# An attention and mixture-of-experts kernel: the weight splits of the first expert in another order around the routing's end, and one running count formed earlier

## The chip, the cores and the metric

One core of a Trainium2 chip runs the whole program. The metric is the device time of one execution in microseconds (us), the median of three runs. For this kernel a change of about 0.2% (1.5 us) is what a measurement can tell from none.

## The reference, cut to what matters

Attention with capped scores feeds a dense layer with SoLU and layer norm, and that feeds a layer of eight experts of which each token uses one. Only the last part lies near the change:

```python
def _moe2_ref(x, modality_id, w_gate, modality_bias, w1, w2):
    logits = x @ w_gate + modality_bias[modality_id]      # x: 1792 x 768, 8 experts
    e_idx = np.argmax(logits, axis=1)
    probs = softmax(logits)
    gate_w = probs[np.arange(N), e_idx]
    for e in range(E):
        mask = e_idx == e
        h = np.maximum(x[mask] @ w1[e], 0.0)              # w1[e]: 768 x 1024
        out[mask] = gate_w[mask, None] * (h @ w2[e])      # w2[e]: 1024 x 768
```

## The kernel before, in words

The 1792 tokens are 14 tiles of 128 (t = 0 to 13). Each tile goes through the dense layer: `m_h` (L590 to L592), `m_act`, `m_tr`, then `m_y` (L645 to L647), which gives y and, in eight more columns, the logits `lg` (L649). `m_out` stores y to `ysc` in memory. Float32 products are made of three passes of TensorE over a high and a low part of each operand. A weight therefore has to be loaded, cast to its high part on ScalarE (`act.copy`) and subtracted to its low part on VectorE (`dve.tensor_sub`); this is called a split.

When the first ten tiles have logits, the expert with most tokens so far is picked (`route_early`), two slots of 128 of its tokens are gathered, and this first expert E is computed while the last tiles are still being routed. Its weights come through `e_weights(w)` (L1021): w = 0 are six blocks of w1, into `winh` and `winl`, w = 1 are eight blocks of w2, into `wouh` and `woul`. Every step of that generator issues one load into a ring of three buffers `e_raw` from SyncE's queue, the cast and the subtraction. The ring makes load k + 3 wait until the subtraction of block k is done. `e_h` (L1032) is the first product of E: 144 matmuls into `e_ph`, with a relu on ScalarE (`e_hh`, L1050) and a low part on VectorE (`e_hl`, L1051) after each quarter of its last pass. `e_o` (L1056) is its second product, into `e_po` (L1063 to L1065).

Meanwhile the routing of tiles 10 to 12 and of tile 13 runs in two generators of `route_group`: a one-hot `r_oh` of each token's expert, a count before each token (matmuls into `pr`), the running count `cum`, the counts of each expert (`route_total`, `route_counts`), then tables of tokens, `route_expert` and `route_end`, which writes `eidx` (the expert of each later slot), `gidx` and `sidx` (its tokens). After that the slots D, H and so on follow (`run_slots`). Their weights are loaded into `raw_D` (a ring of four) on the same queue of SyncE, behind the loads of `e_raw`. The expert index of the first of them is read from `eidx` on SyncE. Between the blocks of `e_o`, TensorE transposes D's gathered tokens (`xtD`, L1209, two buffers in PSUM), which ScalarE and VectorE split (`xh_D` L1210, `xl_D` L1211).

The order on TensorE and VectorE is written out by hand in this part (`manual_schedule`); ScalarE's and SyncE's is chosen by the framework at build time. Each engine executes its list in order. The hand-written order around the change is this (`run` takes steps of the dense layer, `run_h` steps of `e_h`, `ra` and `rb` are the two routings):

```python
        run(3)
        next(rb)
        next(ee["w0"])
        run(4)
        late_w = e_weights(1)
        eh = e_h()
        for k in EHS:
            run_h(k)
            next(rb, None)
            next(late_w)
        for _ in late_w:
            pass
```

Of the kernel before, what the change touches and what calls it, by code (L numbers as in the profile page):

```python
# [12 lines left out]
F16 = mybir.dt.float16  # L13
I32 = mybir.dt.int32
AF = mybir.ActivationFunctionType
ALU = mybir.AluOpType
# [5 lines left out]
NT, DM, DF, NE = 1792, 768, 1024, 8  # L22
P = 128
# [33 lines left out]
PEND0 = 17  # L57
QH = (6, 6)
RDEL = 4
EHS = (8, 22, 20)  # L60
ETD = 8
LSEP = (10, 12)
TRP = (4, 0, 0)
# [23 lines left out]
def attn_moe_kernel(ctx, tc, qt, kt, vv, cap, w_in, w_out, g_ln, ids, w_gate, mbias, w1, w2, out):  # L87
# [164 lines left out]
    def route_group(K, tp, psR, atile, a, b):  # L252
        n = b - a
        oh = K["oh"][:, a:b, :]
        kk = tp.tile([P, n, NE], F32, name=f"kk{a}")
        dve.tensor_tensor(kk, lg[:, a:b, :], nmx[:, a:b].unsqueeze(2).to_broadcast([P, n, NE]), op=ALU.add)
        dve.scalar_tensor_tensor(kk, kk, 0.0, K["rev"][:, a:b, :], op0=ALU.is_equal, op1=ALU.mult)
        fm = tp.tile([P, n], F32, name=f"fm{a}")
        dve.tensor_reduce(fm, kk, axis=AX.X, op=ALU.max)
        dve.tensor_tensor(oh, kk, fm.unsqueeze(2).to_broadcast([P, n, NE]), op=ALU.is_equal)  # L260
        pr = atile(f"pr{a}")[:, 0, :n * NE].rearrange("p (t e) -> p t e", e=NE)
        prev = rstate.get("cum")
        last = b == NTILE
        yield
        mm = []
        if prev is not None:
            mm.append((pr, K["ones"], prev.unsqueeze(1).to_broadcast([P, n, NE])))
        for t in range(n - 1):
            mm.append((pr[:, t + 1:, :], K["ones"], oh[:, t:t + 1, :].to_broadcast([P, n - 1 - t, NE])))
        pe.matmul(pr, K["tri"], oh, start=True, stop=not mm)  # L270
        for i, (o, l, r) in enumerate(mm):
            pe.matmul(o, l, r, start=False, stop=(i == len(mm) - 1))
        cum = tp.tile([P, NE], F16, name=f"cum{a}")
        if n == 1:
            dve.tensor_tensor(cum, prev, oh[:, 0, :], op=ALU.add)
        else:
            cs = tp.tile([P, NE], F32, name=f"cs{a}")
            dve.tensor_reduce(cs, oh.rearrange("p t e -> p e t"), axis=AX.X, op=ALU.add)
            if prev is None:
                dve.tensor_copy(cum, cs)  # L280
            else:
                dve.tensor_tensor(cum, cs, prev, op=ALU.add)
        rstate["cum"] = cum
        if last:
            route_total(K)
        pm = tp.tile([P, n, NE], F32, name=f"pm{a}")
        dve.tensor_tensor(pm, pr, oh, op=ALU.mult)
        if last:
            yield
            route_counts(K, tp)  # L290
            yield
        rf = tp.tile([P, n], F32, name=f"rf{a}")
        dve.tensor_reduce(rf, pm, axis=AX.X, op=ALU.add)
        ri, pl, ph = (tp.tile([P, n], I32, name=f"{x}{a}") for x in ("ri", "pl", "ph"))
        dve.tensor_copy(ri, rf)
        dve.tensor_scalar(pl, ri, P - 1, None, op0=ALU.bitwise_and)
        dve.tensor_scalar(ph, ri, 7, None, op0=ALU.logical_shift_right)
        A, Bm = K["A"][:, a:b, :], K["B"][:, a:b]
        dve.tensor_tensor(A, K["io128"].unsqueeze(1).to_broadcast([P, n, P]),
                          pl.unsqueeze(2).to_broadcast([P, n, P]), op=ALU.is_equal)  # L300
        rm = tp.tile([P, n, NR], F16, name=f"rm{a}")
        dve.tensor_tensor(rm, K["io14"].unsqueeze(1).to_broadcast([P, n, NR]),
                          ph.unsqueeze(2).to_broadcast([P, n, NR]), op=ALU.is_equal)
        dve.tensor_tensor(rm, rm, K["tid"][:, a:b].unsqueeze(2).to_broadcast([P, n, NR]), op=ALU.mult)
        dve.tensor_tensor(Bm, oh.unsqueeze(3).to_broadcast([P, n, NE, NR]),
                          rm.unsqueeze(2).to_broadcast([P, n, NE, NR]), op=ALU.mult)
        if last:
            route_expert(K, tp)
        else:
            yield  # L310
        if a == 0:
            rstate["pt"] = psR.tile([NE * NR, P], F32, name="r_pt")
        for t in range(a, b):
            pe.matmul(rstate["pt"], K["B"][:, t].rearrange("p a b -> p (a b)"), K["A"][:, t, :],
                      start=(t == 0), stop=(t == b - 1), skip_group_check=True)
        if a == 0:
            route_early(K, tp, psR)
        if last:
            yield
            route_end(K, tp)  # L320

    def route_early(K, tp, psR):

# [38 lines left out]
    def route_counts(K, tp):  # L362
        sm = rstate["sm"]
        c8 = tp.tile([NE, 1], F32, name="r_c8")
        dve.scalar_tensor_tensor(c8, rstate["s8"], -float(P), sm[:NE, 0:1], op0=ALU.mult, op1=ALU.add)

        wn = K["wn"]
        dv = tp.tile([NE, 2], F32, name="r_dv")
        nst = tp.tile([NE, 24], F32, name="r_nst")
        for o, lo, hi in ((dv[:, 0:1], 21, 24), (dv[:, 1:2], 14, 21), (wn[:, 6:7], 0, 14)):  # L370
            dve.tensor_scalar(nst[:, lo:hi], K["thr"][:, lo:hi], c8, None, op0=ALU.is_lt, op1=ALU.add, accum_out=o)
        dve.tensor_scalar(wn[:, 7:8], dv[:, 0:1], 4.0, None, op0=ALU.mult)
        dve.tensor_scalar(wn[:, 5:6], dv[:, 1:2], 2.0, None, op0=ALU.mult)
        dve.scalar_tensor_tensor(wn[:, 8:9], dv[:, 0:1], -4.0, wn[:, 5:6], op0=ALU.mult, op1=ALU.add)
        dve.tensor_tensor(wn[:, 9:10], wn[:, 6:7], wn[:, 5:6], op=ALU.subtract)
        dve.scalar_tensor_tensor(wn[:, 10:11], wn[:, 6:7], float(P), c8, op0=ALU.mult, op1=ALU.is_lt)
        dve.tensor_scalar(wn[:, 1:2], dv[:, 0:1], -4.0, None, op0=ALU.mult)
        dve.tensor_copy(wn[:, 4:5], wn[:, 7:8])
        r1, k = wn[:, 7:11], NE * NR
        leq = K["leq"].rearrange("p a b -> p (a b)")  # L380
        pe.matmul(sm[:NE, 8:12], K["lin"], r1, start=True, stop=True)
        pe.matmul(sm[:k, 60:64], K["lex"].rearrange("p a b -> p (a b)"), r1, start=True, stop=False)
        pe.matmul(sm[:k, 60:64], leq, wn[:, 0:4], start=False, stop=True)
        pe.matmul(sm[:k, 64:67], leq, wn[:, 4:7], start=True, stop=True)
        pe.matmul(sm[:1, 72:76], K["one8"], r1, start=True, stop=True)

    def route_expert(K, tp):
        sm = rstate["sm"]
        cmp_ = tp.tile([NE, len(KINDS), NK], F16, name="r_cmp")
        sh = [NE, len(KINDS), NK]  # L390
        dve.tensor_tensor(cmp_, K["io8"], sm[:NE, 8:12].unsqueeze(2).to_broadcast(sh), op=ALU.is_ge)
        pe.matmul(sm[:1, 16:16 + NS], K["ones"][:NE, 0:1], cmp_.rearrange("p a b -> p (a b)"), start=True, stop=True)

    def route_end(K, tp):
        sm = rstate["sm"]
# [11 lines left out]
        t4 = tp.tile([k, 4, TT], F16, name="r_t4")  # L407
        dve.tensor_copy(t4, rstate["pt"][:, :TT].unsqueeze(1).to_broadcast([k, 4, TT]))
        dve.tensor_scalar(eidx, sm[:1, 16:16 + NS], float(NE - 1), None, op0=ALU.min)
        pg, pq = sm[:, 128:128 + NG], sm[:, 192:192 + NK]  # L410
        pe.matmul(pg, tt, selg[:, :NG], start=True, stop=True)
        pe.matmul(pq, t4.rearrange("p a b -> p (a b)"), selg[:, NG:], start=True, stop=True)
# [608 lines left out]
    def e_weights(w):  # L1021

        src, rows, width, hs, ls = ((w1r, DM, DF, winh, winl), (w2r, DF, DM, wouh, woul))[w]
        for k in range(rows // P):
            raw = rt.tile([P, DF], F32, tag="e_raw", name=f"e_raw{w}_{k}", bufs=3)[:, :width]
            sp.dma_start(out=raw, in_=src[ds(ee["reg"] * rows + k * P, P), :])
            h_, l_ = hs[k][:, :width], ls[k][:, :width]
            act.copy(h_, raw)
            dve.tensor_sub(l_, raw, h_)
            yield  # L1030
# [59 lines left out]
    def run(k):  # L1090
        for _ in range(k):
            msteps.pop(0)[1]()

    def run_h(k):
        for _ in range(k):
            next(eh)

    with tc.manual_schedule(engines={ET.PE, ET.DVE}):
        run(4)
        ra, rb = (route_group(K, rt, psR, atile, *x) for x in groups)  # L1100
        next(ra)
        next(ee["w0"])
        run(5)
        next(ra)
        next(ee["w0"])
        run(3)
        next(rb)
        run(3)
        next(ra, None)
        next(ee["w0"])  # L1110
        run(3)
        next(rb)
        next(ee["w0"])
        run(4)
        late_w = e_weights(1)
        eh = e_h()
        for k in EHS:
            run_h(k)
            next(rb, None)
            next(late_w)  # L1120
        for _ in late_w:
            pass
        for _ in eh:
            pass
    for pl_ in (rt, xp, wi, psR):
        pl_.release()
# [469 lines left out]
```

## Time and profile before

| | |
|---|---|
| time, median of 3 runs | 757.17 us (757.06 to 757.83) |
| time of the profiled execution | 758.1 us |
| its span (first to last instruction) | 756.4 us |
| TensorE (PE) busy | 725.8 us, 96% |
| VectorE (DVE) busy | 437.8 us, 58% |
| ScalarE (ACT) busy | 387.1 us, 51% |
| GpSimd (POOL) busy | 116.9 us, 15% |
| moved by DMA | 97.14 MB, mean 128 GB/s |

Between the span and the time of the profiled execution lie 1.7 us in which no instruction of the program runs. Busy time of TensorE includes stretches at half its clock, so a stretch that is busy throughout may still be slow.

### The profile page before, as it was taken

To read this page: it belongs to the slowest core of one execution; us is meant where nothing else is said; L and a number is where in the kernel's file an instruction comes from. 1 tells how busy PE (TensorE), PEld (TensorE's weight loads), DVE (VectorE), ACT (ScalarE), POOL (GpSimd) and SP (SyncE) were. 2 spreads that over 40 slices of the span, in tenths; PEclk is the share of its full clock that TensorE was granted. 3 is DMA by queue.
4 is the path that set the end of the run, shared out by engine and by line. 5 is a ranking of instruction groups with operands and counts; after the bars stand their busy time and mean duration, and the time that the engine had idled before them with its cause. 6 is when DMAs were issued, how large, how long until landed. Compare 5 with 4: busy or idle time off the path is not lost. (4 is left out here: it accounts for less than half of the span.)

```text
span 756.4 us, 11328 instructions
## 1 busy us (share of the span) xinstructions
PE 725.8 (96%) x4302; PEld 558.9 (74%) x4302; DVE 437.8 (58%) x782; ACT 387.1 (51%) x535; POOL 116.9 (15%) x214
## 2 busy tenths in 40 slices
PE   5999999999999999999999998969999999999994
PEld 2443556667767777677698998968879998799983
DVE  7999656756656657555457557546146173563621
ACT  5999756774575555555612234244055162643530
POOL 4221101111021112020032111302210220002010
PEclk9999999999999999999999999979999999999998
DMA  8775121121121110110004012648918359484520
GB/s 290 253 237 197 61 59 43 59 73 43 38 83 37 57 58 13 59 34 13 21 22 148 22 50 98 203 184 301 390 58 273 117 184 404 193 266 171 199 104 23
DMA packets 33426, 97.14 MB, mean 128 GB/s; under 512 B 4903, under 2 KB 11057, under 8 KB 33362
## 3 DMA queue, kind: packets, MB, share of 16 engines
q1 hardware_dynamic: 26546, 66.88, 26.2%
q0 software_dynamic: 6528, 29.42, 11.0%
q8 instruction: 35, 0.57, 0.3%
q14 instruction: 29, 0.24, 0.1%
q10 hardware_dynamic: 288, 0.03, 0.0%
HBM read 85.24 MB, written 11.27 MB: 128 GB/s over the span
## 5 line engine op out<-in xcount | busy, mean ns | idle before, releaser
L730 ACT ACTIVATE e<-sc,sc 112x896 f32<-112x896 f32 x96 | 94.5, 1005 | 67.3 <-PE sc L723 67.3
L735 ACT ACTIVATE e<-e,cap_t 112x896 f32<-112x896 f32 x96 | 98.1, 1045 | 1.7
L765 PE MATMUL av<-e,v 112*64 112x448 f32 x384 | 82.8, 552 | 0.0
L645 PE MATMUL y<-wouh,lh 128*128 128x392 f32 (+1 forms) x224 | 77.9, 348 | 1.6 <-DVE lg L649 1.6
L647 PE MATMUL y<-wouh,ll 128*128 128x392 f32 (+1 forms) x224 | 75.8, 338 | 0.2 <-DVE ll L635 0.2
L646 PE MATMUL y<-woul,lh 128*128 128x392 f32 (+1 forms) x224 | 75.9, 339 | 0.0
L590 PE MATMUL h<-winh,xh 128*128 128x512 f32 x168 | 69.0, 411 | 0.0
L592 PE MATMUL h<-winh,xl 128*128 128x512 f32 x168 | 66.0, 393 | 1.1 <-DVE xl L578 1.1
L591 PE MATMUL h<-winl,xh 128*128 128x512 f32 x168 | 65.6, 390 | 0.0
L645 PEld LDWEIGHTS y<-wouh,lh 128*128 128x128 f32 x224 | 42.0, 188 | 10.3 <-issue 7.1
L765 PEld LDWEIGHTS av<-e,v 112*64 112x64 f32 x384 | 23.3, 136 | 35.4 <-issue 33.4
L1179 DVE TENSOR_TENSOR wl_H<-raw_H,wh_H 128x768 fp32r<-128x768 f32 (+1 forms) x28 | 29.2, 1069 | 32.2 <-ACT wh_H L1178 32.2
L590 PEld LDWEIGHTS h<-winh,xh 128*128 128x128 f32 x168 | 31.6, 188 | 16.4 <-issue 9.3
L1308 PE MATMUL poD<-wh_D,hhD 128*128 128x384 f32 x128 | 43.0, 336 | 0.0
L1309 PE MATMUL poD<-wl_D,hhD 128*128 128x384 f32 x128 | 42.8, 334 | 0.0
L1310 PE MATMUL poD<-wh_D,hlD 128*128 128x384 f32 x128 | 42.8, 334 | 0.0
L647 PEld LDWEIGHTS y<-wouh,ll 128*128 128x128 f32 x224 | 42.1, 188 | 0.8 <-DVE ll L635 0.8
L646 PEld LDWEIGHTS y<-woul,lh 128*128 128x128 f32 x224 | 42.1, 188 | 0.6
L1178 ACT CAST wh_H<-raw_H 128x768 fp32r<-128x768 f32 (+1 forms) x28 | 25.3, 941 | 32.5 <-PE phD L1236 14.1
L1179 DVE TENSOR_TENSOR wl_D<-raw_D,wh_D 128x768 fp32r<-128x768 f32 (+1 forms) x28 | 29.6, 1071 | 18.8 <-ACT wh_D L1178 18.5
L592 PEld LDWEIGHTS h<-winh,xl 128*128 128x128 f32 x168 | 31.5, 188 | 8.8 <-DVE xl L578 2.0
L723 PE MATMUL sc<-qr,kr 64*112 64x448 f32 x128 | 30.4, 601 | 7.8 <-DMA qr<-in_qt_dram 7.8
(373 smaller groups left out, 1604.7 us busy)
## 6 DMA issues: line engine op xcount, KB each, us to landing
rawc<-in_w_out_dram POOLq DMA_DIRECT2D x16, 384.0 KB, 4.1
rawc<-in_w_in_dram POOLq DMA_DIRECT2D x12, 512.0 KB, 4.7
raw_D<-in_w_dram SPq DMA_DIRECT2D x12, 512.0 KB, 5.0
wr_T<-in_w_dram SPq DMA_DIRECT2D x16, 384.0 KB, 6.4
raw_D<-in_w_dram SPq DMA_DIRECT2D x16, 384.0 KB, 5.9
wr_T<-in_w_dram SPq DMA_DIRECT2D x12, 512.0 KB, 7.8
raw_H<-in_w_dram SPq DMA_DIRECT2D x12, 512.0 KB, 5.7
raw_H<-in_w_dram SPq DMA_DIRECT2D x16, 384.0 KB, 3.7
```

Of the source, the lines that this page charges most:

```text
L590: pe.matmul(o, s["xh"][d], winh[d][:, c], start=(d == 0), stop=False)
L591: pe.matmul(o, s["xh"][d], winl[d][:, c], start=False, stop=False)
L592: pe.matmul(o, s["xl"][d], winh[d][:, c], start=False, stop=(d == ND - 1))
L645: pe.matmul(o, s["lh"][f], wouh[f][:, c], start=(f == 0), stop=False)
L646: pe.matmul(o, s["lh"][f], woul[f][:, c], start=False, stop=False)
L647: pe.matmul(o, s["ll"][f], wouh[f][:, c], start=False, stop=(f == NF - 1))
L730: act.activation(e, t[:CK, :, :S], AF.Tanh, scale=sc8[:CK])
L735: act.activation(e, e, AF.Exp, scale=cap_t[:CK])
L765: pe.matmul(o[64 * j:64 * j + 64, :S], v[:, c, 64 * j:64 * j + 64], et[b, p, c][:, j, :], start=(c == 0), stop=(c == 3))
L1179: dve.tensor_sub(l_, raw, h_)
L1308: pe.matmul(p, hh[:, f, o], wh[:, c], start=(f == 0), stop=False)
L1309: pe.matmul(p, hh[:, f, o], wl[:, c], start=False, stop=False)
```

## The change

It does two things. The running count of tile 13 is formed right behind its one-hot, before the routing's first stop, and not after the matmuls that follow. And the steps of the weight splits are taken at other places: the generators of w1 and w2 become one (`weights`), the last three splits of w1 are taken later, w2's first four at or behind the stops of the routing's end, and the other four behind `e_h`. The routing's end has new stops: the sums of `route_counts` are a function of their own (`route_sums`), the matmul of `route_expert` comes after a stop, and `route_end` stops before its two matmuls. `EHS` is now pairs of (steps of `e_h`, splits).

```diff
-EHS = (8, 22, 20)
+EHS = ((8, 1), (16, 1), (18, 3))
...
         last = b == NTILE
+        cum = tp.tile([P, NE], F16, name=f"cum{a}")
+        if n == 1:
+            dve.tensor_tensor(cum, prev, oh[:, 0, :], op=ALU.add)
         yield
...
-        cum = tp.tile([P, NE], F16, name=f"cum{a}")
-        if n == 1:
-            dve.tensor_tensor(cum, prev, oh[:, 0, :], op=ALU.add)
-        else:
+        if n > 1:
...
             yield
-            route_counts(K, tp)
+            r1 = route_counts(K, tp)
             yield
+            route_sums(K, r1)
...
         if last:
-            route_expert(K, tp)
-        else:
-            yield
+            cmp_ = route_expert(K, tp)
+        yield
+        if last:
+            pe.matmul(rstate["sm"][:1, 16:16 + NS], K["ones"][:NE, 0:1], cmp_.rearrange("p a b -> p (a b)"), start=True, stop=True)
...
         if last:
-            yield
-            route_end(K, tp)
+            yield from route_end(K, tp)
...
         dve.tensor_scalar(eidx, sm[:1, 16:16 + NS], float(NE - 1), None, op0=ALU.min)
+        yield
...
+    def weights():
+        yield from ee["w0"]
+        yield from e_weights(1)
...
+        ew = weights()
         next(ra)
-        next(ee["w0"])
+        next(ew)
         run(5)
         next(ra)
-        next(ee["w0"])
         run(3)
         next(rb)
+        next(ew)
         run(3)
         next(ra, None)
-        next(ee["w0"])
         run(3)
         next(rb)
-        next(ee["w0"])
+        next(rb)
+        next(ew)
         run(4)
-        late_w = e_weights(1)
         eh = e_h()
-        for k in EHS:
-            run_h(k)
+        for steps, subs in EHS:
+            run_h(steps)
             next(rb, None)
-            next(late_w)
-        for _ in late_w:
+            for _ in range(subs):
+                next(ew)
+        for _ in eh:
             pass
-        for _ in eh:
+        for _ in ew:
             pass
```

What becomes of it on VectorE where the logits of tile 13 arrive, before and then after the change (`winl3` is the low part of w1's block 3, `e_xl` that of E's tokens, the digits behind an underscore are buffers):

```order
L1029 TENSOR_TENSOR winl3_132<-e_raw0_3_4254,winh3_126 128x1024
L649 SCALAR_TENSOR_TENSOR lg_78<-y13_4215,sm13_4106,bias_t_76 128x8
L651 TENSOR_REDUCE nmx_92<-lg_78 128x1
L256 TENSOR_TENSOR kk13_4269<-lg_78,nmx_92 128x8
L257 SCALAR_TENSOR_TENSOR kk13_4269<-kk13_4269,r_rev_3549 128x8
L259 TENSOR_REDUCE fm13_4272<-kk13_4269 128x1
L260 TENSOR_TENSOR r_oh_3615<-kk13_4269,fm13_4272 128x8
L1011 TENSOR_TENSOR e_xl_4277<-e_xt0_4278,e_xh_4276 128x6x128
...
L1029 TENSOR_TENSOR winl4_133<-e_raw0_4_4308,winh4_127 128x1024
L275 TENSOR_TENSOR cum13_4323<-cum10_4235,r_oh_3615 128x8
```

```order
L654 SCALAR_TENSOR_TENSOR lg_78<-y13_4216,sm13_4106,bias_t_76 128x8
L656 TENSOR_REDUCE nmx_92<-lg_78 128x1
L256 TENSOR_TENSOR kk13_4265<-lg_78,nmx_92 128x8
L257 SCALAR_TENSOR_TENSOR kk13_4265<-kk13_4265,r_rev_3549 128x8
L259 TENSOR_REDUCE fm13_4268<-kk13_4265 128x1
L260 TENSOR_TENSOR r_oh_3615<-kk13_4265,fm13_4268 128x8
L266 TENSOR_TENSOR cum13_4272<-cum10_4211,r_oh_3615 128x8
L1034 TENSOR_TENSOR winl3_132<-e_raw0_3_4274,winh3_126 128x1024
L1016 TENSOR_TENSOR e_xl_4279<-e_xt0_4280,e_xh_4278 128x6x128
```

The logits and the running count `cum13` now stand ahead of the subtraction of w1's block 3, and block 4's has gone to a later place.

On VectorE at the end of `e_h`, before and after (`woul0` to `woul7` are w2's eight blocks, `wl0_D0_0` is the first block of D's weights):

```order
L1029 TENSOR_TENSOR woul4_147<-e_raw1_4_4483,wouh4_139 128x768
L1029 TENSOR_TENSOR woul5_148<-e_raw1_5_4487,wouh5_140 128x768
L1029 TENSOR_TENSOR woul6_149<-e_raw1_6_4491,wouh6_141 128x768
L1029 TENSOR_TENSOR woul7_150<-e_raw1_7_4495,wouh7_142 128x768
L1051 SCALAR_TENSOR_TENSOR e_hl0_4348<-e_ph0_4350,e_hh0_4346 128x512 x2
L1051 SCALAR_TENSOR_TENSOR e_hl1_4349<-e_ph1_4386,e_hh1_4347 128x512 x2
L1179 TENSOR_TENSOR wl0_D0_0_4662<-raw0_D0_0_4651,wh0_D0_0_4661 128x1024
```

```order
L1034 TENSOR_TENSOR woul3_146<-e_raw1_3_4471,wouh3_138 128x768
L1056 SCALAR_TENSOR_TENSOR e_hl0_4358<-e_ph0_4360,e_hh0_4356 128x512 x2
L1056 SCALAR_TENSOR_TENSOR e_hl1_4359<-e_ph1_4397,e_hh1_4357 128x512 x2
L1034 TENSOR_TENSOR woul4_147<-e_raw1_4_4585,wouh4_139 128x768
L1034 TENSOR_TENSOR woul5_148<-e_raw1_5_4589,wouh5_140 128x768
L1034 TENSOR_TENSOR woul6_149<-e_raw1_6_4593,wouh6_141 128x768
L1034 TENSOR_TENSOR woul7_150<-e_raw1_7_4597,wouh7_142 128x768
L1189 TENSOR_TENSOR wl0_D0_0_4662<-raw0_D0_0_4651,wh0_D0_0_4661 128x1024
```

The subtractions of blocks 4 to 7 have moved behind the four low parts `e_hl`; blocks 0 to 3 stand ahead of them.

On ScalarE at the same place, before and after:

```order
L1028 CAST wouh5_140<-e_raw1_5_4487 128x768
L1028 CAST wouh6_141<-e_raw1_6_4491 128x768
L1028 CAST wouh7_142<-e_raw1_7_4495 128x768
L1050 ACTIVATE e_hh0_4346<-e_ph0_4350 128x512 x2
L1050 ACTIVATE e_hh1_4347<-e_ph1_4386 128x512 x2
L1178 CAST wh0_D0_0_4661<-raw0_D0_0_4651 128x1024
```

```order
L1033 CAST wouh5_140<-e_raw1_5_4589 128x768
L1033 CAST wouh6_141<-e_raw1_6_4593 128x768
L1055 ACTIVATE e_hh0_4356<-e_ph0_4360 128x512 x2
L1055 ACTIVATE e_hh1_4357<-e_ph1_4397 128x512 x2
L1033 CAST wouh7_142<-e_raw1_7_4597 128x768
L1188 CAST wh0_D0_0_4661<-raw0_D0_0_4651 128x1024
```

Only the cast of block 7 has moved behind the relus `e_hh`; those of blocks 4 to 6 stand ahead of them as before. On SyncE the eight loads of w2 still stand ahead of D's loads `raw_D`; the reading of `eidx` has moved from behind load 4 to ahead of load 3.

## Rows read from the trace of the kernel before

**Rows 1.** TensorE's waits over the span: us in total, times, longest.

```profile
PE e_po L1063 <- ACT e_hh L1050: 6.1, 1, 6.1
PE y L645 <- DVE lg L649: 1.6, 1, 1.6
PE poH L1310 <- PEq L1548: 1.1, 1, 1.1
...
PE r_sm L360 <- DVE cum L275: 1.1, 1, 1.1
```

**Rows 2.** Timeline of TensorE: start, us, work, idle before it and its releaser.

```profile
491.59 0.28 PE L1047 MATMUL e_ph<-e_xh,winl 128*128 128x256 f32 x1
497.98 0.69 PE L1063 MATMUL e_po<-wouh,e_hh 128*128 128x384 f32 x1 [6.12 <-ACT e_hh L1050]
...
511.08 1.01 PE L1209 MATMUL xtD<-ident,ygD 128*128 128x128 f32 x6 [0.62 <-DVE xl_D L1211]
```

**Rows 3.** Stretches: busy of PE, PEld, DVE, ACT, POOL; granted clock, DMA share, GB/s.

```profile
491.80:498.00 6.20, 0.09 (x2) 0.02 (x1) 2.45 (x3) 2.79 (x4) 0.00 (x0) 0.69 1.02 370
498.00:504.40 6.40, 6.31 (x23) 5.80 (x24) 2.41 (x4) 1.19 (x2) 0.00 (x0) 0.50 0.32 127
504.40:506.60 2.20, 2.20 (x16) 2.20 (x15) 0.47 (x1) 1.10 (x2) 0.00 (x0) 0.99 0.00 0
...
496.70:500.30 3.60, 2.23 (x7) 1.72 (x8) 1.56 (x2) 1.23 (x2) 0.00 (x0) 0.50 0.90 360
```

**Rows 4.** Timeline of ScalarE, 491 to 509 us.

```profile
491.60 0.83 ACT L1028 CAST wouh<-e_raw 128x768 fp32r<-128x768 f32 x1 [7.85 <-DMA e_raw<-in_w_dram]
...
496.60 0.83 ACT L1028 CAST wouh<-e_raw 128x768 fp32r<-128x768 f32 x1 [3.01 <-DMA e_raw<-in_w_dram]
497.34 0.59 ACT L1050 ACTIVATE e_hh<-e_ph 128x512 fp32r<-128x512 f32 x1
...
505.99 2.93 ACT L1178 CAST wh_D<-raw_D 128x1024 fp32r<-128x1024 f32 x3
```

**Rows 5.** Timeline of VectorE, 467 to 512 us.

```profile
467.67 1.22 DVE L1029 TENSOR_TENSOR winl<-e_raw,winh 128x1024 fp32r<-128x1024 f32 x1
...
480.09 0.16 DVE L398 TENSOR_TENSOR r_at<-r_sm,r_ck 112x4 f32<-112x4 f32 x1 [1.26 <-PE r_sm L392]
...
481.37 0.17 DVE L409 TENSOR_SCALAR eidx<-r_sm 1x32 int32<-1x32 f32 x1
...
484.36 2.69 DVE L1029 TENSOR_TENSOR woul<-e_raw,wouh 128x768 fp32r<-128x768 f32 x3
...
498.34 0.68 DVE L1051 SCALAR_TENSOR_TENSOR e_hl<-e_ph,e_hh 128x512 fp32r<-128x512 f32 x1
...
506.13 0.69 DVE L1051 SCALAR_TENSOR_TENSOR e_hl<-e_ph,e_hh 128x512 fp32r<-128x512 f32 x1 [2.76 <-ACT e_hh L1050]
507.06 3.50 DVE L1179 TENSOR_TENSOR wl_D<-raw_D,wh_D 128x1024 fp32r<-128x1024 f32 x3 [0.24 <-ACT wh_D L1178]
510.48 1.01 DVE L1211 TENSOR_TENSOR xl_D<-xtD,xh_D 128x384 fp32r<-128x384 f32 x2
```

**Rows 6.** Issues on SyncE's queue (block 5, block 7, D's first); POOL's first gather.

```profile
485.35 0.33 SPq L1026 DMA_DIRECT2D e_raw<-in_w_dram  x1
...
487.08 1.62 SPq L1026 DMA_DIRECT2D e_raw<-in_w_dram  x1
488.91 0.84 SPq L1165 DMA_DIRECT2D raw_D<-in_w_dram  x1
...
483.27 1.10 POOL L1187 DMA_INDIRECT ygD<-ysc,gidx  x1 [5.72 <-DVE r_sf L416]
```

**Rows 7.** Single loads, KB and us to landing, issued at 473.3, 485.4 and 508.3.

```profile
e_raw<-in_w_dram SPq DMA_DIRECT2D x1, 384.0 KB, 2.9
...
e_raw<-in_w_dram SPq DMA_DIRECT2D x1, 384.0 KB, 6.2
...
raw_D<-in_w_dram SPq DMA_DIRECT2D x1, 512.0 KB, 3.5
```

More of the change, by code (lines that the diff above doesn't have):

```diff
@@ L378, in route_counts, with route_sums @@
         dve.tensor_copy(wn[:, 4:5], wn[:, 7:8])
-        r1, k = wn[:, 7:11], NE * NR
+        return wn[:, 7:11]
+    def route_sums(K, r1):
+        sm, wn, k = rstate["sm"], K["wn"], NE * NR
         leq = K["leq"].rearrange("p a b -> p (a b)")
@@ L391, in route_expert @@
         dve.tensor_tensor(cmp_, K["io8"], sm[:NE, 8:12].unsqueeze(2).to_broadcast(sh), op=ALU.is_ge)
-        pe.matmul(sm[:1, 16:16 + NS], K["ones"][:NE, 0:1], cmp_.rearrange("p a b -> p (a b)"), start=True, stop=True)
+        return cmp_
     def route_end(K, tp):
```

## The prediction

> **What bounds the kernel now.** I read TensorE's waits first, because TensorE is busy for 96% of the span and a change can only win what it waits for, or what it runs slowly. Four waits lie in the stretch that the change touches: 1.6 us before the last part of y, which ends when VectorE has formed the logits, 1.1 us for the running count, 6.1 us before the first matmul of `e_po` [rows 1], and 0.6 us before the second group of D's transposes `xtD` [rows 2]. Behind 511 us there is only one more wait, of 1.1 us in the last slot's `poH` [rows 1], which the change does not touch. So whatever TensorE is late or early by at 511 us stays to the end: I forecast the moment of that second `xtD` group and carry the difference over.
>
> The long wait has a price beside its 6.1 us. TensorE stops at 491.87 and goes on at 497.98 [rows 2], and from then to 504.4 its granted clock is 0.50, that is 1.2 and not 2.4 GHz; it does 23 matmuls in those 6.4 us, and then 16 in 2.2 us at the upper level [rows 3]. At that later rate the 23 would take 3.2 us, so the lower clock took some 3.1 us.
>
> Next, why it waits. The relu `e_hh` runs at 497.34 on ScalarE, straight behind the cast of w2's block 7, and the casts of blocks 5 and 7 each wait for their load (7.9 and 3.0 us) [rows 4]. ScalarE works its list in order, so a relu whose input is ready at 491.9 stands behind weights that `e_o` needs only much later. Last, SyncE's queue: D's first load is issued at 488.91, right behind block 7's at 487.08 [rows 6].
>
> **The change, part by part.** *The front.* The logits stood behind a subtraction of 1.22 us [rows 5], and now stand ahead of it: the wait of 1.6 falls to 0.5. The running count is formed right behind the one-hot: the wait of 1.1 goes, but the transposes' low part `e_xl` is now behind that subtraction, and `pr` needs its buffer, which gives 0.1 to 0.2 back. Together 2.1 us, so TensorE reaches the end of its `e_h` work at 489.8 and not 491.87. This is no gain by itself, since what follows is a wait that ends with a load.
>
> *The routing's end.* On VectorE `eidx` was written at 481.37, behind four subtractions and a wait of 1.26 us for the small matmul [rows 5]. Now three subtractions of w1 (1.2 each) stand between the logits and `eidx`, in place of two of them and two of w2 (0.9 each, three in 2.69 us [rows 5]), and the matmul is ready. That is 1.1 + 1.8 + 1.0 (most of the wait) less 1.2: `eidx` is written 2.6 us earlier, ending at 478.9. POOL's gathers of D's tokens, at 483.27 before [rows 6], move up about 3 us. TensorE's order of the small matmuls costs nothing, as it finds their inputs ready.
>
> *The splits of w2.* Load 3 now follows the reading of `eidx` and block 0's subtraction, so it goes out at 479.9. It lands 3.4 us later: one load alone took 2.9, one beside the gathers 6.2 [rows 7], and this one meets only the first gather. Cast 0.8 [rows 4] and subtraction 0.9 free the buffer for load 6 at 485.2. Load 6 runs amid the gathers as block 5's did at 485.35, which took 6.2 us [rows 6, 7]: 491.4. The relu stands behind that cast still: cast to 492.2, relu to 492.8. TensorE goes on at 492.8 and not 497.98: 5.2 us earlier, after a wait of 3.0 us. Bounds for the landing: 4.6 us if the fewer bytes tell (D's loads no longer compete), 7.2 if the gathers, now more at the same time, tell more; so 491.2 to 493.8.
>
> Of this landing a page has another price. The Trainium skill (DMA: Bandwidth & Descriptors, Queues, rings and completion order) says that each DMA engine takes packets in turn from the queues that have work. By that, half of the 370 GB/s [rows 3] for SyncE's queue brings blocks 4 to 6 (1.18 MB) in 6.4 us from about 484, and the time would come out 1 us lower, 758.9. The trace is rougher: 6.2 us for a load with little else in its own queue.
>
> *What is moved behind the relus.* Here the ring and the queue bite. Load 7 waits for block 4's subtraction, and that now stands behind all four `e_hl`, which need TensorE's last matmuls of `e_h`. D's loads stand behind load 7 in SyncE's queue, though their buffers are free. Before, block 4's subtraction was the third of the row at 484.36, and `raw_D` left at 488.91 [rows 5, 6]. Now: from TensorE's resumption at 497.98 to the end of the last `e_hl` (506.82) passed 8.84 us [rows 2, 5]; 0.4 of it was block 7's subtraction, which is gone. So 8.4 at the lower clock throughout; at the upper clock 6.0, since of the 3.1 us some 0.7 hides behind the first relu and low part. A wait of 3.0 lies between one that left the clock up (1.6) and one that lowered it (6.1) [rows 1, 3]: I take the middle, 7.2. Then block 4's subtraction with its hand-over, 1.0, and load 7 goes at 501.0, D's first at 501.6, almost 13 us later than before.
>
> From load 7's issue, the third of D's blocks lands after 7.0 us: 2.9 for 384 KB alone [rows 7], then 3 x 524 kB at 360 to 400 GB/s (360 in the stretch at 496.7 [rows 3]), 4.1. ScalarE casts D's blocks 0 to 2 before it touches `xtD`, and VectorE subtracts them before `xl_D` [rows 4, 5], so the last cast (1.0), subtraction (1.2) and half of the 1.01 us of `xl_D` follow, with 0.1 of hand-over: 2.8. Only then has the second `xtD` group a free buffer in PSUM. Total 9.8, bounds 9.1 and 10.5.
>
> **The sum.** 492.8 + 7.2 + 1.0 + 9.8 = 510.8, against 511.08 before: 0.3 us earlier. All that is won ahead of `e_h` and before `e_po` is given back, as TensorE gets to that `xtD` group at about 503.7 (12.5 us after resuming before, less the clock) and waits 7.1 us. That wait is longer than the 6.1 us after which the clock was lowered for 6.4 us of work, a loss of 3.1. This new price has the bounds 0 (no lowering) and 3.1; the row is so near that I take 3.0. So the profiled execution goes from 758.1 to 760.8 (span 756.4 to 759.1), and the median, 0.9 below the profiled execution, from 757.17 to 759.9: slower by 2.7 us, or 0.36%. The bound of what can be told is 1.5 us.
>
> The rest of the chain keeps its distance: D's blocks 3 to 5 land no later relative to `xtD` than before, and load 7 itself is needed only by the last eighth of `e_o`. If that cover failed, each us would add one.
>
> **Rivals.** *No change.* Blocks 4 to 6 land early (TensorE resumes at 491.2) and the short wait leaves the clock up: 491.2 + 6.0 + 1.0 + 9.8 = 508.0, 3.1 earlier, less 3.0 for the clock in the second wait: 757.1. For it: no D load competes with block 6. Against: the 6.2 us row was slowed mostly by gathers.
>
> *Faster.* The same, but the wait before `xtD` costs only itself, because TensorE's clock is not lowered in it or recovers within 1 us: 3.1 won less 0.5, 754.6. It decides once the clock's price in that second wait is under 1.6 us and resumption at or before 491.2; against it stands the lowering after 6.1 us.
>
> *Both waits at the lower clock, loads late.* 492.8 + 8.4 + 1.0 + 10.5 = 512.7, 1.6 later, and 3.1 for the second lowering: 761.9.
>
> *That the change doesn't do what it says*: on ScalarE only block 7's cast passes the relus, not four. This is known from the built order and in the sum; four would let TensorE resume at 490.4.
>
> **How the numbers follow.** Forecast 0.50 (its own range 758.7 to 761.5), late loads with both lowerings 0.15, no change 0.22, faster 0.13. The range for 8 in 10 leaves out most of the faster case and the tail of the slowest: 756.0 to 762.0. Faster by over 0.2%: 0.13; within: 0.22; slower: 0.65.
>
> **What would show it.** In the changed kernel's profile the wait for `e_hh` should be near 3 us, those for `lg` and `cum` 0.5 and gone, and a new wait of about 7 us should stand before `xtD` L1219, ended by VectorE's `xl_D`; `raw_D` should be issued near 501.6 behind block 7's load, and a stretch of clock 0.5 should follow. The forecast fails if `raw_D` is issued early after all, if that `xtD` group doesn't wait for it, or if the clock stays up.

## The result, and the profile after

The changed kernel takes 764.62 us (764.21 to 765.30 in four runs) beside 757.5 us for the kernel before on the same chip, a ratio of 1.0093 (95% interval 1.0076 to 1.0111): slower by 7.1 us, where 2.7 were forecast. The range ended at 762.0. Run again beside other kernels it took 763.35 us against 757.57, 1.0091 (1.0071 to 1.0110).

The profiled execution took 764.74 us, its span is 763.0 us; before it was 756.4. TensorE's waits over the span (us in total, times, longest), which answer to [rows 1]:

```profile
PE xtD L1219 <- DVE xl_D L1221: 8.5, 1, 8.5
...
PE e_po L1068 <- ACT e_hh L1055: 4.8, 1, 4.8
PE poH L1320 <- PEq L1558: 1.1, 1, 1.1
...
PE y L650 <- DVE lg L654: 0.5, 1, 0.5
```

The wait for the running count is gone, that for the logits fell from 1.6 to 0.5, that for the relu from 6.1 to 4.8. A new one, the longest of the program, stands before `xtD`. The four together were 9.4 us and are now 13.8.

To set the two traces side by side one needs a common zero. TensorE stops for the logits at 469.08 − 1.62 = 467.46 in the profile of before and at 469.11 − 0.49 = 468.62 in that of after, so after is 1.16 us late ahead of the waits that the change touches. TensorE's timeline, first the row of before and then of after (start, us, work, idle before it and its releaser):

```profile
469.08 0.44 PE L645 MATMUL y<-wouh,lh 128*128 128x384 f32 x1 [1.62 <-DVE lg L649]
```

```profile
469.11 0.44 PE L650 MATMUL y<-wouh,lh 128*128 128x384 f32 x1 [0.49 <-DVE lg L654]
...
495.74 0.69 PE L1068 MATMUL e_po<-wouh,e_hh 128*128 128x384 f32 x1 [4.82 <-ACT e_hh L1055]
...
515.52 1.54 PE L1219 MATMUL xtD<-ident,ygD 128*128 128x128 f32 x6 [8.45 <-DVE xl_D L1221]
```

The lateness lies near the start. Stretches of after (busy time of PE, PEld, DVE, ACT, POOL; granted clock, DMA share, GB/s), then the same stretches of the second profile of the same program:

```profile
25.00:27.00 2.00, 2.00 (x12) 0.48 (x12) 1.97 (x5) 2.00 (x5) 0.38 (x1) 0.65 1.03 381
27.00:29.00 2.00, 2.00 (x10) 0.45 (x4) 1.90 (x10) 0.84 (x1) 0.15 (x1) 0.50 0.70 235
```

```profile
25.00:27.00 2.00, 2.00 (x17) 0.33 (x13) 1.97 (x5) 2.00 (x4) 0.50 (x1) 1.00 1.04 395
27.00:29.00 2.00, 2.00 (x15) 0.94 (x11) 1.90 (x10) 1.69 (x3) 0.04 (x1) 1.00 0.77 230
```

One execution falls to 0.50 there and does 22 matmuls in 4 us, the other at 1.00 does 32; the profile of before is at 1.00 there too. It is the same program, so this difference is not the change. The second profile stops for the logits at 466.96, 0.50 us ahead of before, so the start alone moves by 1.66 us between executions. Below, 1.16 us are taken off the times of after before they are compared.

Now SyncE's queue and ScalarE, which answer to [rows 6] and [rows 4]. Issues of load 6, load 7 and D's first:

```profile
485.65 0.33 SPq L1031 DMA_DIRECT2D e_raw<-in_w_dram  x1
...
504.40 0.33 SPq L1031 DMA_DIRECT2D e_raw<-in_w_dram  x1
...
504.94 0.33 SPq L1175 DMA_DIRECT2D raw_D<-in_w_dram  x1
```

ScalarE's timeline: the cast of block 6 and the relu, then block 7 and D's blocks 0 to 2:

```profile
494.36 0.83 ACT L1033 CAST wouh<-e_raw 128x768 fp32r<-128x768 f32 x1 [1.68 <-DMA e_raw<-in_w_dram]
495.10 0.59 ACT L1055 ACTIVATE e_hh<-e_ph 128x512 fp32r<-128x512 f32 x1
...
507.43 0.83 ACT L1033 CAST wouh<-e_raw 128x768 fp32r<-128x768 f32 x1 [4.74 <-DMA e_raw<-in_w_dram]
508.78 1.05 ACT L1188 CAST wh_D<-raw_D 128x1024 fp32r<-128x1024 f32 x1 [0.52 <-DMA raw_D<-in_w_dram]
511.43 1.04 ACT L1188 CAST wh_D<-raw_D 128x1024 fp32r<-128x1024 f32 x1 [1.61 <-DMA raw_D<-in_w_dram]
512.70 1.04 ACT L1188 CAST wh_D<-raw_D 128x1024 fp32r<-128x1024 f32 x1 [0.22 <-DMA raw_D<-in_w_dram]
```

Each of these casts waits for a transfer; only the relu does not. How load 6 landed, beside the last of three loads in a row before the change: first the landing of block 7's load in the kernel before (KB, us), then what the queues of POOL (q0) and SyncE (q1) moved in the changed kernel from 483.4 to 494.36 (packets, MB, share of the 16 engines), and the last two stretches ahead of the cast of block 6:

```profile
e_raw<-in_w_dram SPq DMA_DIRECT2D x1, 384.0 KB, 9.5
```

```profile
q0 software_dynamic: 352, 1.69, 49.2%
q1 hardware_dynamic: 434, 1.18, 28.6%
```

```profile
492.00:493.00 1.00, 0.00 (x0) 0.00 (x0) 0.00 (x0) 0.68 (x1) 0.00 (x0) 1.00 0.46 167
493.00:494.36 1.36, 0.00 (x0) 0.00 (x0) 0.00 (x0) 0.00 (x0) 0.00 (x0) 0.59 0.06 25
```

VectorE (as [rows 5]) ends the last `e_hl` at 503.42, subtracts blocks 4 to 6 and then waits three times for ScalarE's casts, that is for the loads:

```profile
502.73 0.69 DVE L1056 SCALAR_TENSOR_TENSOR e_hl<-e_ph,e_hh 128x512 fp32r<-128x512 f32 x1 [1.97 <-ACT e_hh L1055]
503.33 2.68 DVE L1034 TENSOR_TENSOR woul<-e_raw,wouh 128x768 fp32r<-128x768 f32 x3
508.29 0.96 DVE L1034 TENSOR_TENSOR woul<-e_raw,wouh 128x768 fp32r<-128x768 f32 x1 [2.27 <-ACT wouh L1033]
509.86 1.23 DVE L1189 TENSOR_TENSOR wl_D<-raw_D,wh_D 128x1024 fp32r<-128x1024 f32 x1 [0.60 <-ACT wh_D L1188]
512.51 2.50 DVE L1189 TENSOR_TENSOR wl_D<-raw_D,wh_D 128x1024 fp32r<-128x1024 f32 x2 [1.43 <-ACT wh_D L1188]
514.92 1.01 DVE L1221 TENSOR_TENSOR xl_D<-xtD,xh_D 128x384 fp32r<-128x384 f32 x2
```

So the second `xtD` group starts at 515.52, and TensorE's clock is lowered once more (as [rows 3]):

```profile
495.74:500.07 4.33, 4.33 (x17) 4.10 (x18) 1.37 (x3) 1.19 (x2) 0.00 (x0) 0.50 0.01 2
515.52:520.55 5.03, 5.02 (x18) 5.03 (x19) 3.92 (x7) 1.90 (x3) 0.00 (x0) 0.50 0.20 80
520.55:522.75 2.20, 2.20 (x17) 2.16 (x16) 1.07 (x3) 1.58 (x3) 0.00 (x0) 1.00 0.48 135
```

**The sum of the two profiles.** The last `e_hl` ends at 506.82 before [rows 5] and at 503.42 − 1.16 = 502.26 after: 4.6 us won. From there to the second `xtD` group pass 4.26 us before (to 511.08 [rows 2]) and 515.52 − 503.42 = 12.10 after: 7.8 us lost. From that group to the end of the span pass 756.4 − 511.08 = 245.3 before and 763.0 − 515.52 = 247.5 after: 2.2 lost to the clock. That is 5.4 us, and with the 1.16 from the start the 6.6 by which the spans differ. The same sum with the second profile, whose span is 760.4, gives 5.2 won, 8.0 and 1.7 lost: 4.5 us.

These intervals are what the experiments were read by:

| kernel (us) | wait for `e_hh` | last `e_hl` to second `xtD` group | wait there | group to end of span |
|---|---|---|---|---|
| before | 6.1 | 4.26 | 0.6 | 245.3 |
| after | 4.8 | 12.10 | 8.5 | 247.5 |
| after, second profile | 4.5 | 12.23 | 8.6 | 247.0 |
| deferral alone | 1.4 | 12.13 | 8.5 | 247.4 |
| loops exchanged | 5.6 | 4.27 | 0.6 | 245.6 |
| block 4 ahead | 5.6 | 6.53 | 2.9 | 246.7 |
| block 4 ahead, ScalarE by hand | 0.7 | 6.65 | 3.0 | 246.2 |
| the same, blocks 5 to 7 in `e_o` | 0.7 | 4.26 | 0.6 | 245.6 |
| after, ScalarE by hand | 0.7 | 12.30 | 8.6 | 247.0 |
| after, with further matmuls | 4.9 | 11.65 | 0.4 | 245.4 |

All are worked out from rows like those above.

### The profile page after: what moved, and what is told of

It is laid out like the page before. It is cut to its first block, busy times and chain, and to the rows that moved or that the text cites. A ratio compares the mean times of both kernels' runs of the same rounds, so it can differ in the third digit from the quotient of the medians.

```text
span 763.0 us, 11321 instructions
## 1 busy us (share of the span) xinstructions
PE 728.3 (95%) x4302; PEld 560.6 (73%) x4302; DVE 438.5 (57%) x782; ACT 387.2 (51%) x535; POOL 117.1 (15%) x214
## 3 DMA queue, kind: packets, MB, share of 16 engines
q0 software_dynamic: 6528, 29.42, 10.9%
## 5 line engine op out<-in xcount | busy, mean ns | idle before, releaser
L1188 ACT CAST wh_D<-raw_D 128x768 fp32r<-128x768 f32 (+1 forms) x28 | 26.0, 931 | 23.6 <-DMA raw_D<-in_w_dram 23.4
```

## The experiments

Theory: load 7 waits for block 4's subtraction, which the change put behind the last `e_hl`; D's loads stand behind load 7 in SyncE's queue; so `xtD` waits and the clock is lowered again. Rivals: the earlier routing and its gathers, or the wait for the relu that stayed.

**1. The deferral alone**, in the kernel before:

```diff
-        for _ in late_w:
+        next(late_w)
+        for _ in eh:
             pass
-        for _ in eh:
+        for _ in late_w:
             pass
```

> The kernel before with one part of the change alone: w2's splits 4 to 7 are taken behind e_h; the front and the routing's end stay as they were. Main theory (load 7 waits for block 4's subtraction, that stands behind the last e_hl, and D's loads stand behind load 7 in SyncE's queue): TensorE resumes near 495.0 instead of 497.98, because the relu now stands behind block 6's cast only; the last e_hl ends 7.7 us later, load 7 goes out near 503.7, the second xtD group starts 11.1 us behind that, near 514.8 against 511.08, with a wait of about 8 us and a second stretch at clock 0.5 that costs 2.2 us: 763 us. Rival (the earlier routing and gathers are what made the changed kernel slow): the splits alone change little, 757 us or less.

Measured: 761.89 us against 757.6, 1.0055 (1.0030 to 1.0079), 1.1 us under what was expected. TensorE resumes at 494.33 after 1.4 us and waits 8.5 us before the second `xtD` group at 514.04. The wait and the second lowering come with the deferral and need nothing else of the change.

**2. The two last loops exchanged** in the changed kernel, so that the splits stand ahead of the rest of `e_h`:

```diff
-        for _ in eh:
+        for _ in ew:
             pass
-        for _ in ew:
+        for _ in eh:
             pass
```

> The changed kernel with its last two loops exchanged, so that all splits of w2 stand ahead of the rest of e_h again; the front and the routing's end stay changed. On ScalarE the first relu of e_hh then stands behind block 6's cast and ahead of block 7's, the others behind block 7's. Main theory: D's loads leave SyncE's queue before 491 us, no new wait stands before xtD, and only one stretch at clock 0.5 is left: 754 to 757 us, no slower than before. Rival (the moves in the routing's end cost the time): near 764 us.

Measured: 757.36 us against 757.6, 0.9997 (0.9980 to 1.0013), just above the expected range. Its waits:

```profile
PE e_po L1068 <- ACT e_hh L1055: 5.6, 1, 5.6
...
PE e_ph L1048 <- DVE e_hl L1056: 1.3, 1, 1.3
...
PE xtD L1219 <- DVE xl_D L1221: 0.6, 1, 0.6
```

The whole loss is gone, with the front and the routing's end still changed: the rival falls. The earlier front gave nothing that this measurement can tell either; its interval still holds a gain of up to 1.5 us.

**3. The running count alone**, in the kernel before:

```diff
         last = b == NTILE
+        cum = tp.tile([P, NE], F16, name=f"cum{a}")
+        if n == 1:
+            dve.tensor_tensor(cum, prev, oh[:, 0, :], op=ALU.add)
         yield
...
-        cum = tp.tile([P, NE], F16, name=f"cum{a}")
-        if n == 1:
-            dve.tensor_tensor(cum, prev, oh[:, 0, :], op=ALU.add)
-        else:
+        if n > 1:
```

> The kernel before with the other part of the change alone: the running count is formed beside its one-hot. The wait of 1.1 us for it goes, TensorE ends its e_h work about 1 us earlier and waits as much longer for the relu, since that ends with a load: 757.2 us, no change. Rival (the front's gain reaches the end): 756 us.

Measured: 756.90 us against 756.92, 0.9999 (0.9984 to 1.0015). That is no change, though a gain of 1 us, which the rival expected, is within the interval. Its profile (754.98 us, the shortest of twelve runs) does not show the expected reason:

```profile
PE e_po L1063 <- ACT e_hh L1050: 4.9, 1, 4.9
...
PE r_sm L381 <- DVE r_wn L378: 0.7, 1, 0.7
```

The wait of 1.1 us for the count is gone, but 0.7 come back as a wait for `r_wn`, so TensorE ends its `e_h` work only 0.4 us earlier, counted from its stop for the logits. The wait for the relu did not grow: it is 4.9 us beside 6.1, since block 7's load took 8.4 us here (486.26 to 494.61) and not 9.5. That the front's gain is waited away before the relu is therefore not shown.

**4. ScalarE's order by hand too**, in the changed kernel:

```diff
-    with tc.manual_schedule(engines={ET.PE, ET.DVE}):
+    with tc.manual_schedule(engines={ET.PE, ET.DVE, ET.Activation}):
```

> The changed kernel with ScalarE's order in this part written by hand too, so that the casts of w2's blocks 4 to 7 really stand behind the four relus; block 4's subtraction stays behind the e_hl. Main theory: TensorE resumes near 492 us (by the changed kernel's clockless front) and not 495.74, with its clock at 1.00; the last e_hl ends near 498, load 7 goes out near 499, and the second xtD group follows 11.1 us later, near 510, after a wait that still is some 7 us and lowers the clock: 515.5 less 510.1 is 5.4 us, so 759 us, still slower than before. Rival (the forecast's 9.8 us from load 7 to xtD holds once fewer transfers run together): 758 us. Rival (the wait for the relu was the whole cost): 755 us or less.

Measured: 760.58 us against 756.92, 1.0057 (1.0036 to 1.0078). The relu's wait is down to 0.7 us and the clock stays at 1.00 there, and the kernel is still slower than before: its `xtD` group starts at 512.26 after 8.6 us. I had expected 510 and a time of 759 us; by hand the front is slower (its wait for the logits is 1.4 us, not 0.5). The wait for the relu was not what cost the time.

**5. Further matmuls in the wait** before `xtD`:

```diff
+            if f == LTR[1]:
+                spare = atile("e_spare")
+                for _ in range(44):
+                    pe.matmul(spare[:, 0, :HD], ee["hh"][0][:, 0, :P], wouh[0][:, :HD], start=True, stop=True)
             if f in LTR:
                 tr(LTR.index(f))
```

> The changed kernel with 44 further matmuls (128x384, into a PSUM buffer that nobody reads) ahead of the second xtD group, in the stretch in which TensorE waits there; at 0.17 us each they take 7.6 of the 8.5 us. Main theory (the clock goes to its lower level because TensorE stands still): no stretch at clock 0.5 follows the xtD group, and the 2.2 us that it costs come off: 762.4 us. Rival (the lower clock has another cause): the stretch stays, 764.6 us; or the matmuls delay the group, more than that.

Measured: 761.0 us against 756.92, 1.0073 (1.0051 to 1.0095), 1.4 us under what was expected. In its timeline and stretches:

```profile
505.50 7.80 PE L1538 MATMUL e_spare<-wouh,e_hh 128*128 128x384 f32 x44
...
513.65 1.01 PE L1219 MATMUL xtD<-ident,ygD 128*128 128x128 f32 x6 [0.36 <-DVE xl_D L1221]
```

```profile
505.70:513.65 7.95, 7.60 (x44) 7.27 (x42) 5.16 (x6) 5.69 (x7) 0.00 (x0) 1.00 0.92 336
513.65:518.00 4.35, 4.35 (x29) 4.16 (x30) 4.10 (x8) 2.77 (x6) 0.00 (x0) 1.00 0.32 111
```

The clock stays at 1.00, and the rest of the program takes 245.4 us instead of 247.5 (247.0 in the second profile), as before the change. So the lowering comes from TensorE's standing still, and its price behind this wait is 2.1 us (1.6 by the second profile). The group itself starts no earlier: it waits for the loads.

**6. Two of D's four gathers left out**, so that D's last two tiles use the tokens of its first two:

```diff
         for i, c in enumerate(cols(s)):
+            if s == STATIC[0] and i > 1:
+                gs.append(gs[i - 2])
+                continue
             g = g2.tile([P, YW], F32, tag="yg", name=f"yg{sname(s)}_{i}", bufs=4)
```

> The changed kernel without two of D's four gathers (tiles 2 and 3 of slot D read the tokens of tiles 0 and 1, so the output of those tokens is another), 0.8 MB less that shares the DMA engines with the loads of w2's blocks 4 to 6. If the gathers are what stretched load 6 from the forecast 6.2 to 8.7 us: it lands some 2.5 us earlier, TensorE resumes near 493.5, load 7 and the second xtD group move by 2 us, near 762.5 us. Rival (the three loads hold up one another in SyncE's queue): load 6 lands less than 0.7 us earlier, 764 us or more.

Measured: 760.65 us against 756.92, 1.0054 (1.0034 to 1.0073), less than either theory expected. Load 6 goes out at 485.34, and its cast follows block 5's:

```profile
492.48 0.83 ACT L1033 CAST wouh<-e_raw 128x768 fp32r<-128x768 f32 x1 [0.33 <-DMA e_raw<-in_w_dram]
```

It starts 7.1 us behind the issue, against 494.36 − 485.65 = 8.7 in the changed kernel: the two gathers explain 1.6 of the 2.5 us by which the forecast of 6.2 was short (1.2 beside the second profile, where load 6 took 8.3). That lies between what the two theories expected for the landing. That the rest is the loads in one another's way is not shown.

**7. Block 4's split ahead of the rest of `e_h`**:

```diff
-EHS = ((8, 1), (16, 1), (18, 3))
+EHS = ((8, 1), (16, 1), (18, 4))
```

> The changed kernel with one number altered: the split of w2's block 4 is taken ahead of the rest of e_h too, so that load 7 no longer waits for the e_hl; the splits 5 to 7 stay behind. Main theory: load 7 goes out near 490.5 us and D's loads right behind it; TensorE resumes near 495.7 as in the changed kernel, reaches the second xtD group near 507 and waits there for 1.5 us at most, and the second lowering of the clock is gone: 7 to 8 us come off the 515.5 of that group and 2.2 us off the clock, less what the relu behind block 7's cast costs, 753 to 756 us. Rival (the xtD group waits for D's tokens or for ScalarE's and VectorE's work and not for the queue): the wait stays above 5 us and the time near 763.

Measured: 758.19 us against 757.6, 1.0012 (0.9994 to 1.0031). Load 7 goes out at 490.77 and D's first at 491.31, the wait before `xtD` falls from 8.5 to 2.9, and nearly all of the loss comes back. But I had expected 753 to 756. TensorE resumes late, at 496.52, since load 6, now with load 7 and D's loads behind it in the queue, took 9.4 us (485.71 to 495.14). VectorE shows why 2.9 us are left:

```profile
503.13 0.69 DVE L1056 SCALAR_TENSOR_TENSOR e_hl<-e_ph,e_hh 128x512 fp32r<-128x512 f32 x1 [1.71 <-ACT e_hh L1055]
503.74 2.69 DVE L1034 TENSOR_TENSOR woul<-e_raw,wouh 128x768 fp32r<-128x768 f32 x3
506.34 3.49 DVE L1189 TENSOR_TENSOR wl_D<-raw_D,wh_D 128x1024 fp32r<-128x1024 f32 x3
509.74 1.02 DVE L1221 TENSOR_TENSOR xl_D<-xtD,xh_D 128x384 fp32r<-128x384 f32 x2
```

No wait for a load stands in this chain. The deferred subtractions themselves, 2.69 us, now lie between the last `e_hl` and `xl_D`. The deferral has a second price, which in the changed kernel hides under the late loads.

**8. The same with ScalarE's order by hand** (the edits of 4 and 7 together), so that the casts of blocks 5 to 7 stand behind the relus:

> As the kernel with block 4's split ahead, and ScalarE's order in this part written by hand like TensorE's and VectorE's, so that the casts of blocks 5 to 7 stand behind all four relus. Main theory: the relu waits for block 4's load alone (it landed at 488.7 in the changed kernel), TensorE resumes near 492 after a wait near 1 us that leaves its clock at 1.00, and D's loads go out near 491: the second xtD group starts near 505, when xl_D has passed the casts and subtractions of blocks 5 to 7 and of D's 0 to 2. Against 511.08 before (512.2 with the later front of the changed kernel's profile) that is 7 us: 750.5 us. Rival (D's blocks land so late that xtD waits anyway, with a lowered clock): 755 us or more.

Measured: 753.9 us against 757.6, 0.9955 (0.9942 to 0.9969), faster than before, but 3.4 us short of what I expected: the wait before `xtD` is 3.0 us, again with the three subtractions in front.

**9. Blocks 5 to 7 in `e_o`**: as 8, with these blocks loaded behind D's first four into another ring and split between D's transposes.

```diff
-        for k in range(rows // P):
+        for k in range((ND, 5)[w]):
...
             if f in LTR:
                 tr(LTR.index(f))
+            if f + 2 in raw:
+                act.copy(wouh[f + 2][:, :DM], raw[f + 2])
+                dve.tensor_sub(woul[f + 2][:, :DM], raw[f + 2], wouh[f + 2][:, :DM])
 
+        raw = {}
+        for k in range(5, NF):
+            raw[k] = g2.tile([P, DM], F32, tag="tm", name=f"e_late{k}", bufs=NTM)
+            sp.dma_start(out=raw[k], in_=w2r[ds(ee["reg"] * DF + k * P, P), :])
         late["ps"] = psT
```

> As the kernel with ScalarE's order by hand and block 4's split ahead, but w2's blocks 5 to 7 are loaded behind D's first four, into another ring, and cast and subtracted in e_o between D's transposes (ahead of its steps 5 to 7), not in front of D's blocks 0 to 2. If the 3.0 us before xtD that were left there are VectorE's three subtractions of 0.9 us, which stand between the last e_hl and D's: the second xtD group follows the last e_hl by 4.3 us, as in the kernel before (506.82 to 511.08), and not by 6.65; the wait falls to about 0.6 us, the stretch at clock 0.5 behind it goes, and the time falls from 753.9 to 751 us. Rival (D's blocks land late): the wait stays above 2 us and the time at 753.5 or more.

Measured: 750.4 us (748.54 to 752.65) against 757.57, 0.9909 (0.9889 to 0.9929): the best of all, 7 us ahead of the kernel before. VectorE goes from the last `e_hl` straight to D's blocks:

```profile
498.48 0.69 DVE L1056 SCALAR_TENSOR_TENSOR e_hl<-e_ph,e_hh 128x512 fp32r<-128x512 f32 x1 [1.87 <-ACT e_hh L1055]
499.41 3.50 DVE L1189 TENSOR_TENSOR wl_D<-raw_D,wh_D 128x1024 fp32r<-128x1024 f32 x3 [0.24 <-ACT wh_D L1188]
502.82 1.01 DVE L1221 TENSOR_TENSOR xl_D<-xtD,xh_D 128x384 fp32r<-128x384 f32 x2
```

The 4.26 us are those of the kernel before, the clock is at 1.00 throughout this part, and of the three waits 1.4, 0.7 and 0.6 us are left.

**10. D's ring with three buffers**, in the changed kernel:

```diff
-NRAW = 4
+NRAW = 3
```

> The changed kernel with D's ring of loads at three buffers in place of four, in all slots, so its time as a whole says little. It prices one term: from load 7's issue to the second xtD group. If the fourth load of D, in flight with the first three, is what makes D's third block land 8.3 us behind load 7's issue and not the forecast 7.0: it lands about 7.0 us behind it, and the xtD group 9.8 us. Rival (the loads are slow one by one): 8 us or more, and 11.

Measured in a single run, 765.08 us: the fourth load goes out only at 509.87, but the cast of D's third block still begins 8.6 us behind load 7's issue (502.26 to 510.85) and the group starts 11.4 us behind it, at 513.68. Taking the fourth load away did not bring the block earlier. Its stretches show the end of the transfers:

```profile
507.00:509.00 2.00, 0.00 (x0) 0.00 (x0) 0.61 (x2) 1.04 (x1) 0.00 (x0) 0.71 0.96 352
509.00:510.00 1.00, 0.00 (x0) 0.00 (x0) 0.84 (x1) 0.45 (x1) 0.00 (x0) 0.50 0.38 136
510.00:510.90 0.90, 0.00 (x0) 0.00 (x0) 0.28 (x1) 0.64 (x2) 0.00 (x0) 0.50 0.07 21
```

The block lands at the end of two stretches in which the DMA engines are busy for 38% and 7% only, so almost all of its bytes had moved a microsecond earlier. The gather `ygT` also fell into these transfers here, so the run does not price the term cleanly.

**11. The changed kernel again**, unedited:

> The changed kernel once more, beside the two that follow. The deferral alone gave 761.9 us and the further matmuls 761.0, which leaves 2.7 us between the deferral and the whole change that no view of their profiles shows: both resume within 0.3 us of each other and wait 8.5 us before xtD. If executions differ that much (in some profiles TensorE's clock is at 0.50 for some 3 us near 27 us, in others not), the changed kernel comes out nearer to the deferral alone, 761 to 763 us. Rival (the front and the routing's end add a cost of their own once the splits are deferred): 764 us or more again.

Measured: 763.35 us, between the two expectations. Its profile (762.09 us, the shortest of its five runs) has the clock at 1.00 near 27 us, resumes at 493.74 and waits 8.6 us.

## Why the prediction was wrong in size

The direction and the chain were as forecast: the waits for the logits and the count fell, ScalarE's relu still stood behind block 6, load 7 left behind block 4's subtraction, D's loads stood behind load 7, a wait as long as or longer than the one removed stood before `xtD`, and the clock was lowered a second time. Experiments 1, 2, 5 and 7 show the links from block 4's subtraction on. Step by step, with 1.16 us taken off:

- *TensorE's end of `e_h` work* 489.8: measured 490.92 − 1.16 = 489.8. *`eidx`* 478.9: 479.90 − 1.16 = 478.7. Right.
- *"Load 6 runs amid the gathers as block 5's did ..., which took 6.2 us"*: this is the step that failed most. It left 0.7 us earlier than forecast (485.65 − 1.16, not 485.2) but took 8.7, above the bound of 7.2. The row was the wrong one: block 5 was the first of three loads that left in a row, load 6 is the last of three. The kernel before had such a last one, block 7's load at 487.08 [rows 6], and it took 9.5 us to land; four of D's loads stood behind it, so it is a bound and not a copy. In the changed kernel the gathers, 3 us earlier as forecast (the first at 481.38 − 1.16, not 483.27 [rows 6]), met loads 4, 5 and 6: the three got 1.18 MB in 10.9 us, or 108 GB/s, and the last 1.4 of these brought almost nothing. What holds up that end stays open. Two gathers less, and load 6 took 7.1; with load 7 and D's loads behind it (experiment 7), it took 9.4. TensorE resumes at 494.6 and not 492.8: 1.8 us. The Trainium skill (DMA: Bandwidth & Descriptors, Queues, rings and completion order) says that the engines take packets in turn from the queues with work. The estimate that the prediction worked out from it, 6.4 us for blocks 4 to 6 from about 484, missed by more than the forecast: they took from 483.45 to 494.36.
- *Resumption to the last `e_hl`* 7.2: measured 503.42 − 495.74 = 7.68, 0.5 more; the clock was at 0.50 for the first 4.3 us of it.
- *Block 4's subtraction with its hand-over* 1.0: 504.40 − 503.42 = 0.98. Right.
- *"From load 7's issue ... Total 9.8, bounds 9.1 and 10.5"*: measured 11.1, again above the bound, 1.3 us. The third block's cast begins 8.3 us behind load 7's issue and not 7.0. A mean rate of 360 to 400 GB/s held for the stretch, but a block is there when the last of its rows is. In experiment 10, with no load right behind it, the block lands after a microsecond in which little moves; why that end takes so long stays open. Holding back the fourth load did not shorten it.
- *The second lowering* 3.0: measured 2.2 from the spans and 2.1 against experiment 5, so 0.8 less (1.7 and 1.6 with the second profile).

1.8 + 0.5 + 1.3 − 0.8 = 2.8 on top of the forecast 2.7 is the 5.4 us of the profiles, within rounding. The rival "both waits at the lower clock, loads late" was nearest, with the sizes still larger; the faster one and that of no change needed load 6 to land early. The rest up to the 7.1 of the medians (5.8 in the second comparison) is not located. The first profile's 1.16 us at the start are of that kind, but the same stretch at 0.50 is in the profiles of faster kernels too (experiments 2, 8 and 9) and not in the second one of the changed kernel, so it can't be put down to the change. That the deferral alone measured 2.7 us less than the whole change in its first runs and 1.5 less than in the second has no wait to show for it, and its interval (1.0030 to 1.0079) overlaps theirs.

One price I had not seen at all: the deferred subtractions, which are VectorE's time between the last `e_hl` and `xl_D`. Under the late loads it cost nothing, so it was not in the error; in experiments 7 and 8 the three that were left there were the next bound, and 9 took them away.

## What to carry to other kernels

Work that is put off keeps its buffer, and the queue behind that buffer: before a split is moved behind something late, look up which load waits for its ring and what else stands behind that load. Then ask the same of the engine's own list: the gap into which the work is moved may be the path of the next stage. A landing time is better bounded by the longest row seen with the same neighbours (here 9.5 us and not 6.2), plus what the change brings closer, than by the rate of a busy stretch.

## What was not expected of the hardware

- After a wait of 0.7 us the granted clock stayed at 1.00 (experiments 4, 8, 9). In the deferral alone, after a wait of 1.4 us, it still fell to 0.50 from about 495.4 to 498.8, one us after TensorE had resumed. After 2.9 us it was 0.50 for some 3 us, which cost about 1 us; after 8.5 us for about 10, half of it in the wait.
- Three loads of 384 KB in one queue beside D's gathers took 5.3, 7.5 and 8.7 us to land in the changed kernel, while one with nothing ahead of it in the queue took 3.0. In the last 1.4 us before the third landed, the DMA engines were busy for 6%.
- The same program ran near 27 us at 0.50 in one profile and at 1.00 in another.
